# Order of two early loads and number of first spins in a fused cosine attention and MLP kernel

## The chip, the core and the metric

The kernel runs on one core of a Trainium2 chip. A core has four compute engines with instruction streams of their own: TensorE (PE; its weight loads are listed as PEld), VectorE (DVE), ScalarE (ACT) and GpSimd (POOL). SyncE (SP) only issues transfers. Each engine takes its instructions in the order in which the program issued them. Transfers run on the core's 16 DMA engines, whoever issued them. Those that POOL issues form the software queue, q0 in the profile; those of SP form a hardware queue, q1. The metric is the device time of one execution in microseconds (us), and smaller is better.

## The reference

Cosine attention over 8 batches with 12 heads, 448 positions and a head width of 64, then an MLP with the exact GELU:

```
q_n = q / (norm(q) + 1e-6);  k_n = k / (norm(k) + 1e-6)
scores = q_n @ k_n^T / tau            # tau = 0.1
attn = softmax(scores);  x = attn @ v # heads side by side: 3584 x 768
out = gelu(x @ w_in) @ w_out          # w_in 768 x 2048, w_out 2048 x 768
```

All inputs and the output are float32.

## The kernel before

Four heads of one batch make a quad; each batch has three quads, and there are 24 in all. For a quad, q and k come in as one tile of 448 KB each (`load_qk`, issued on SP, L129). Their squares are taken (`square`, L154 on ACT or L156 on POOL), summed over a head's width on VectorE (`reduce`, L165), turned into inverse norms (`logs` and `roots` on ACT, `inverses` with `rn` on VectorE, L192), and q and k are scaled by them into the bf16 tile `qkb` (`scale`, L208, mostly on POOL). `qkb` has to be transposed for the scores. The first five units (those of batch 0 and the first of batch 1) are transposed on PE into PSUM (`transposes`, tile `tp`, L225) and copied out by VectorE (`copies`, L230). From batch 1's second quad on, a DMA transpose issued by SP does it (L220). Then come the scores (`scores`, tile `st`, L246, PE), their exps (`exps`, tile `pt`, L253, ACT), the row sums and the products with v (`sums` L266 and L275, `values` L289, PE), and the division on VectorE that leaves `x` (L297 to L323). The exps need no maximum, since a cosine over tau is at most 10.

The MLP follows batch by batch. `first(b)` (L648) multiplies x by w_in (tile `hp`, L660) and ACT applies GELU (L695). The second product, with w_out (tile `op`, L352), is cut into single matmuls by `second_pieces` (L343). They are put into a list, `fill`, and `attention(b, fill)` (L596) takes them out in runs between the attention steps of the next batch; for batch 1 the runs are 20, 13, 14, 17, 16 and 16 matmuls long. For batch 0 the list is sorted so that the first 48 matmuls need only columns 0 to 383 of w_out, and the next 48 only columns 384 to 767.

Quad 0 is split into two units of two heads, so that its first scores can start before the rest is loaded. v comes in parts: quad 0 alone, quads 1 and 2 together, and then batch by batch (`load_v`, L137, transfer in L141). w_in comes in four blocks of rows and columns, each as two transfers (`load_wi`, L382, transfers in L387). Its first block holds rows 0 to 255 with all columns. w_out comes in four quarters (`load_wo`, L391, transfer in L394). All of these convert float32 to bf16 on the way, and POOL issues them all. Each `upto(f, n)` issues those of the first n calls of f that have not been issued yet.

The order of the first batch is written out by hand in `attention_first` (L411). It decides the order of each engine's instructions, and for POOL also when each load is issued. `spin(n)` (L406) issues n matmuls of a blank tile that nobody reads; they keep PE at work where it would wait. A spin uses the same PSUM tiles, in turn, as the transposes (`mm_tile`, L99), so a spin behind the transposes waits until the copy has read that tile. The 20 spins of L721 are the first PE work, ahead of the first transposes.

One load is held back by hand. In `first(0)`, behind the sixth GELU, POOL copies one column of the first tile that a DMA transpose has filled (`held`, L706 and the line behind it), and only then issues the last quarter of w_out (rows 1024 to 2047 of columns 384 to 767).

The lines around the change are these; quad 0's first unit is `0` and k is part `1`:

```python
        scale(0, ((DV, 1),))
        scale(0, ((GP, 0),))
        reduce(1, K)
        transposes(0, 1)
        upto(load_wi, 1)
        transposes(0, 0)
...
        copies(0, 0)
        upto(load_v, 2)
        roots(1)
```

Of the kernel before, what the change touches and what calls it, by code (L numbers as in the profile page):

```python
# [16 lines left out]
def kernel(  # L17
# [81 lines left out]
    def mm_tile(name, shape=(128, 512), dtype=F32, aside=None):  # L99
        t = ps_mm.tile(list(shape), dtype, tag=f"mm{turn[0] if aside is None else turn[0] ^ aside}", name=name)  # L100
        if aside is None:
            turn[0] ^= 1
        return t
# [54 lines left out]
    def reduce(u, part=slice(0, 2)):  # L158
        g, s0, s1 = units[u]
        sq = sq_t[g][:, :, s0:s1]  # L160
        n, j = place[u]
        if n not in nq_t:
            nq_t[n] = nrm.tile([128, len(groups[n]), 2, s1 - s0, C], F32, tag="nq", name=f"nq{n}")
        nq = nq_t[n][:, j]
        nc.vector.tensor_reduce(nq[:, part], sq[:, part], mybir.AxisListType.X, ALU.add)  # L165
# [8 lines left out]
    def roots(n):  # L174
        ln = ln_t.pop(n)
        if n <= NQ:
            sr_t[n] = root2[n % len(root2)][:, :math.prod(shapes[n])]
            nc.scalar.activation(sr_t[n][:, :, 0], ln.rearrange("p j i s c -> p (j i s c)"), AF.Exp, scale=0.5)
        else:
            sr_t[n] = nrm.tile(list(ln.shape), F32, tag="sr", name=f"sr{n}")  # L180
            nc.scalar.activation(sr_t[n], ln, AF.Exp, scale=0.5)  # L181
# [32 lines left out]
    def transposes(u, i=None):  # L214
        g, s0, s1 = units[u]
        qkb = qkb_t[g]
        if g not in qkT_t:
            qkT_t[g] = qkTp.tile([128, 2, C, 128], BF16, tag="qkT", name=f"qkT{g}")
        if i is None:
            nc.sync.dma_start_transpose(out=qkT_t[g].rearrange("p i c s -> p (i c) s"),  # L220
                                        in_=qkb.rearrange("p i c s d -> p (i c s d)"))
            return
        tp = tp_t[u, i] = mm_tile(f"tp{u}_{i}", (128, C, 128), BF16)
        for c in range(C):
            nc.tensor.transpose(tp[64 * s0:64 * s1, c, :], qkb[:, i, c, s0:s1].rearrange("p s d -> p (s d)"), ident)  # L225

    def copies(u, i):
        g, s0, s1 = units[u]
        rows = slice(64 * s0, 64 * s1)
        nc.vector.tensor_copy(qkT_t[g][rows, i], tp_t.pop((u, i))[rows])  # L230
# [169 lines left out]
    def upto(f, n, last=None):  # L400
        last = {load_qk: NG, load_v: NV, root: len(groups), load_wi: NQ + 1, load_wo: 4}.get(f, NU)
        while done.get(f, 0) < min(n, last):
            done[f] = done.get(f, 0) + 1
            f(done[f] - 1)

    def spin(n):  # L406
        ps = ps_mm.tile([128, 512], F32, tag=f"mm{turn[0]}", name="spin")
        for _ in range(n):
            nc.tensor.matmul(ps[:, :S], lhsT=ident, rhs=blank, start=True, stop=True)  # L409

    def attention_first():  # L411
# [15 lines left out]
        scale(0, ((GP, 0),))  # L427
        reduce(1, K)
        transposes(0, 1)
        upto(load_wi, 1)  # L430
        transposes(0, 0)
        logs(1)
        copies(0, 1)
        square(2, ((AC, Q),))
        copies(0, 0)
        upto(load_v, 2)
        roots(1)
        square(2, ((AC, K),))
        inverses(1)
# [278 lines left out]
    upto(load_qk, 1)  # L718
    nc.scalar.preload_act_table_set(EXP_SET)
    upto(load_qk, 3)  # L720
    spin(20)  # L721

    late = nrm.tile([128, 1], F32, tag="late", name="late", bufs=1)
    nc.gpsimd.tensor_copy(late, qk_t[0][:, 1, 1, C - 1, D - 1:D])
# [3 lines left out]
    for b in range(B):  # L728
        if b == 0:
            attention_first()  # L730
            acc.close()
            third.append(ctx.enter_context(tc.tile_pool(name="ps_third", bufs=1, space=bass.MemoryType.PSUM)))
        else:
            attention(b, fill)
        first(b)
        sb, hf = divmod(b, 2)
        todo = [(t, ni) for t in (range(3) if hf == 0 else range(3, 7)) for ni in range(2)]
        if b == 0:
            todo.sort(key=lambda x: x[1])
        tail = [2 * S // 128 - 1] if b == B - 1 else []  # L740
        fill = [f for t, ni in todo if t not in tail for f in second_pieces(sb, t, ni)]
        fill += [f for t in tail for f in last_pieces(sb, t)]
# [37 lines left out]
```

## Time and profile before

| | |
|---|---|
| median of 4 runs | 414.2 us (414.04 to 414.36) |
| the profiled execution | 414.23 us, one of these runs |
| its span, first to last instruction | 412.4 us |
| ACT busy, share of the span | 248.5 us, 60% |
| POOL busy, share of the span | 167.4 us, 41% |
| granted PE clock, mean over the span | 1.00 |
| time to landing, v of quad 0 | 7.7 us |
| time to landing, v of quads 1 and 2 | 15.5 us |
| time to landing, w_in's first block, two transfers | 8.1 and 10.6 us |
| time to landing, last quarter of w_out | 8.2 us |

The profile is one execution of the program on the chip. A row of its timeline has the start, the time, the engine, the line and the operation, the tiles that are written and read, the shapes, and how many such instructions follow each other. In brackets stands how long the engine had been idle before them, and what released it. An engine name with a q at its end (SPq) is the sequencer, which issues transfers. A row of the chain has the start, the time and what was done; the chain is followed back from the last instruction, at each step to what released it. A row of the DMA queues has the number of packets, the megabytes and the share of the 16 engines' time in the window that was asked for. A share above 100% means that packets overlap on an engine.

The time to landing runs from the start of the issue to the end of the transfer. Matmul ends are modelled, so the starts of matmuls are the better guide.

### The profile page before, as it was taken

How to read it: one execution, taken by the hardware profiler on the slowest of the kernel's cores; microseconds unless marked ns; L12 is line 12 of the kernel's file. 1: busy time of each engine (PE TensorE's matmuls, PEld its weight loads, DVE VectorE, ACT ScalarE, POOL GpSimd, SP SyncE). 2: the span in 40 equal slices, each digit the busy share in tenths (PEclk: the TensorE clock that was granted, in tenths of full speed). 3: DMA queues.
4: the chain of work that ended last, by engine and by line, in shares of the span. 5: the costliest groups of instructions: out<-in, count | busy, mean ns of one | idle time of the engine just before them, and what ended most of it. 6: DMA issues, size and time to landing. Idle time of an engine off the chain costs nothing.

```text
span 412.4 us, 8277 instructions
## 1 busy us (share of the span) xinstructions
PE 406.2 (98%) x3505; PEld 212.5 (52%) x3505; DVE 189.0 (46%) x381; ACT 248.5 (60%) x364; POOL 167.4 (41%) x116
## 2 busy tenths in 40 slices
PE   7999999999999999999999999999999999999996
PEld 3445555555555555555555555555555555555564
DVE  5785316931278222943158331773128611481021
ACT  5996696577656567664664658646665457754300
POOL 4995655093900928053720628227360233000000
PEclk9999999999999999999999999999999999999999
DMA  8999999852495507943495332965088130610033
GB/s 287 262 256 213 202 197 288 210 134 46 83 241 166 135 0 115 276 77 121 36 230 185 79 95 52 217 185 133 2 150 212 38 46 2 121 40 2 0 78 77
DMA packets 66484, 54.53 MB, mean 132 GB/s; under 512 B 38672, under 2 KB 62352, under 8 KB 66448
## 3 DMA queue, kind: packets, MB, share of 16 engines
q1 hardware_dynamic: 54464, 41.79, 40.1%
q0 software_dynamic: 11600, 11.80, 18.1%
q8 instruction: 27, 0.44, 0.4%
q10 hardware_dynamic: 384, 0.43, 0.3%
q14 instruction: 9, 0.07, 0.1%
HBM read 45.61 MB, written 11.01 MB: 137 GB/s over the span
## 4 chain that ended last, share of the span: by engine, by line
PE 95%; POOL 2%; DMA 1%; DVE 0%; ACT 0%; issue 0%; POOLq 0%
PE hp L660 35%; PE op L352 35%; PE st L246 9%; PE o L289 8%; PE sm L275 4%; PE op L371 1%; PE sm L266 1%; POOL qkb L208 1%; DMA qk<-in_q_dram 1%; PE tp L225 1%; POOL wi L387 1%; DVE nq L165 0%; PE spin L409 0%; POOL v L141 0%; ACT sq L154 0%
## 5 line engine op out<-in xcount | busy, mean ns | idle before, releaser
L253 ACT ACTIVATE pt<-st 128x896 bf16<-128x896 f32 x168 | 142.7, 916 | 65.9 <-PE st L246 65.5
L352 PE MATMUL op<-wo,g 128*128 128x384 bf16 x864 | 147.8, 327 | 0.0
L660 PE MATMUL hp<-x,wi 128*128 128x448 bf16 x768 | 146.9, 353 | 0.0
L352 PEld LDWEIGHTS <-g 128*128 128x128 bf16 x864 | 81.5, 98 | 62.0 <-issue 10.6
L660 PEld LDWEIGHTS <-wi 128*128 128x128 bf16 x768 | 74.4, 98 | 71.4 <-issue 3.0
L695 ACT ACTIVATE g<-hp 128x448 bf16<-128x448 f32 x128 | 65.4, 545 | 67.8 <-PE hp L660 67.6
L208 POOL TENSOR_TENSOR qkb<-qk,rn 128x896 bf16<-128x896 f32 (+1 forms) x49 | 79.6, 1647 | 40.7 <-DVE rn L192 40.7
L165 DVE TENSOR_REDUCE nq<-sq 128x28 f32<-128x1792 f32 (+2 forms) x30 | 48.7, 1634 | 50.4 <-POOL sq L156 47.7
L356 DVE COPY ot<-op 128x384 f32<-128x384 f32 x54 | 29.5, 547 | 88.0 <-PE op L352 86.0
L156 POOL TENSOR_TENSOR sq<-qk 128x1792 f32<-128x1792 f32 (+1 forms) x22 | 66.5, 3035 | 4.8 <-DMA qk<-in_k_dram 4.8
L190 POOL TENSOR_SCALAR se<-sr 128x28 f32<-128x28 f32 (+1 forms) x16 | 4.8, 298 | 125.8 <-ACT sr L181 125.8
L246 PE MATMUL st<-qkT 64*64 64x448 bf16 x672 | 47.5, 357 | 0.1
L289 PE MATMUL o<-pt,v 64*64 64x448 bf16 x672 | 37.7, 353 | 0.0
L192 DVE RECIPROCAL rn<-se 128x28 f32<-128x28 f32 (+2 forms) x20 | 7.1, 354 | 57.2 <-POOL se L190 57.0
L246 PEld LDWEIGHTS <-qkT 64*64 64x64 bf16 x672 | 18.6, 105 | 22.9 <-issue 14.3
L318 DVE STREAM_TRANSPOSE rs<-rc 128x448 f32<-128x448 f32 x48 | 28.4, 625 | 0.8
L323 DVE TENSOR_TENSOR x<-o,rs 128x448 bf16<-128x448 f32 x48 | 27.2, 599 | 0.6
L289 PEld LDWEIGHTS <-v 64*64 64x64 bf16 x672 | 17.7, 106 | 17.6 <-issue 9.0
L297 DVE STREAM_TRANSPOSE tr<-sm 128x448 f32<-128x448 f32 x24 | 15.5, 646 | 13.6 <-PE sm L275 11.1
L275 PE MATMUL sm<-pt,ones 128*32 128x448 bf16 (+1 forms) x336 | 17.8, 332 | 0.0
L309 DVE TENSOR_REDUCE tr<-tr 32x28 f32<-32x28 f32 x84 | 16.5, 196 | 1.6
L409 PE MATMUL spin<-blank,ident 128*128 128x448 bf16 x33 | 9.8, 447 | 2.2 <-DVE root L89 1.9
(44 smaller groups left out, 119.5 us busy)
## 6 DMA issues: line engine op xcount, KB each, us to landing
qk<-in_q_dram SPq DMA_DIRECT2D x23, 448.0 KB, 6.6
qk<-in_k_dram SPq DMA_DIRECT2D x23, 448.0 KB, 8.5
out_dram<-ot SPq DMA_DIRECT2D x48, 192.0 KB, 3.6
v<-in_v_dram POOLq DMA_DIRECT2D x7, 672.0 KB, 12.4
wo<-in_moe_w_out_dram POOLq DMA_DIRECT2D x4, 768.0 KB, 13.8
wi<-in_moe_w_in_dram POOLq DMA_DIRECT2D x4, 512.0 KB, 13.2
out_dram<-ot SPq DMA_DIRECT2D x12, 96.0 KB, 2.2
wi<-in_moe_w_in_dram POOLq DMA_DIRECT2D x4, 256.0 KB, 16.1
```

What stands on the lines that cost most here:

```text
L156: eng.tensor_tensor(sq[:, part], t[:, part], t[:, part], ALU.mult)
L165: nc.vector.tensor_reduce(nq[:, part], sq[:, part], mybir.AxisListType.X, ALU.add)
L208: eng.tensor_tensor(qkb[:, i, :, s0:s1].rearrange("p c s d -> p s c d"), t[:, i, s0:s1], rn[:, i].to_broadcast([128, s1 - s0, C, D]), ALU. ...
L246: nc.tensor.matmul(st[cols, n, :S], lhsT=qkT[rows, 1, c, cols], rhs=qkT[rows, 0, :, cols], start=True, stop=True, tile_position=(64 * s, 6 ...
L253: nc.scalar.activation(pt[:, :m], st[:, :m, :S], AF.Exp, scale=inv_tau)
L275: nc.tensor.matmul(bank_t[g, "sm"][r:r + 32, cols], lhsT=ones, rhs=pt_t[g, s, c][:, cols], start=(c < 2), stop=(c >= C - 2), tile_position ...
L289: nc.tensor.matmul(bank_t[g, h][cols, :S], lhsT=v_t[g][rows, s, c, :], rhs=pt_t[g, s, c][rows], start=(c == 0), stop=(c == C - 1), tile_po ...
L318: nc.vector.transpose(rs, bank_t[g, "rc"][:, h].to_broadcast([128, NB, 32]))
L352: nc.tensor.matmul(ps[:, :NH], lhsT=g_t[sb][:, kf, t * 128:(t + 1) * 128], rhs=wo[:, kf, ni * NH:(ni + 1) * NH], start=(kf == 0), stop=(kf ...
L356: nc.vector.tensor_copy(ot[:, ni * NH:(ni + 1) * NH], ps[:, :NH])
L660: nc.tensor.matmul(hps[m], lhsT=wi[:, kd, m * 128:(m + 1) * 128], rhs=x_t[b][:, kd, :], start=(kd == 0), stop=(kd == KD - 1))
L695: nc.scalar.activation(g_t[sb][:, m, hf * S:(hf + 1) * S], hps.pop(m), AF.Gelu)
```

## The change

Two lines of the hand-written program are different, in two places. In `attention_first`, the load of v for quads 1 and 2 is issued just ahead of the first block of w_in; before, it was issued three program lines behind the second transposes, and behind that block on POOL. In the body of the kernel the first burst of spins has 17 matmuls and not 20.

```diff
@@ attention_first
         reduce(1, K)
         transposes(0, 1)
+        upto(load_v, 2)
         upto(load_wi, 1)
         transposes(0, 0)
         logs(1)
         copies(0, 1)
         square(2, ((AC, Q),))
         copies(0, 0)
-        upto(load_v, 2)
         roots(1)
         square(2, ((AC, K),))
         inverses(1)
@@ body of the kernel
     upto(load_qk, 1)
     nc.scalar.preload_act_table_set(EXP_SET)
     upto(load_qk, 3)
-    spin(20)
+    spin(17)
```

Everything else is the same, on every engine.

## Prediction

> **What bounds the kernel now.** I read the page first: engine totals and the chain that ended last.
>
> ```profile
> span 412.4 us, 8277 instructions
> PE 406.2 (98%) x3505; PEld 212.5 (52%) x3505; DVE 189.0 (46%) x381; ACT 248.5 (60%) x364; POOL 167.4 (41%) x116
> ...
> PE 95%; POOL 2%; DMA 1%; DVE 0%; ACT 0%; issue 0%; POOLq 0%
> ```
>
> TensorE (PE) carries 95% of the chain. What another engine can still give lies at the start, so next I asked for the chain in order of time from 0 to 70 us.
>
> ```profile
> 6.97 1.36 POOL qkb L208
> 8.33 1.21 POOL wi L387 x2
> 9.54 0.78 POOL v L141
> 10.32 0.30 issue
> 10.66 1.83 POOL qkb L208 x2
> 12.49 1.20 POOL wi L387 x2
> 13.86 1.70 POOL qkb L208
> 15.60 0.56 PE tp L225 x7
> ```
>
> Up to 15.60 the chain is GpSimd's (POOL's); from there it is PE to the end. POOL stood still from 10.32 to 10.66, and again for 0.16 us before 13.86 (both times until VectorE's `rn`, says the timeline). Then the timeline from 0 to 11 us, engine by engine, for who holds `rn`:
>
> ```profile
> 1.93 6.49 PE L409 MATMUL spin<-blank,ident 128*128 128x448 bf16 x20 [1.93 <-DVE root L89]
> 8.47 0.94 PE L225 MATMUL tp<-ident,qkb 128*64 128x128 bf16 x14
> 9.06 1.15 DVE L230 COPY qkT<-tp 64x896 bf16<-64x896 bf16 x2 [1.00 <-PE tp L225]
> 10.87 0.92 ACT L253 ACTIVATE pt<-st 128x896 bf16<-128x896 f32 x1 [0.68 <-PE st L246]
> ```
>
> PE is in the spins until 8.42 and transposes at 8.47, although VectorE had the scaled k at 7.54 (row 6.91 + 0.63) and POOL the scaled q at 8.33. VectorE waits 1.00 us for the transposes, ScalarE (ACT) 0.68 us for the scores behind them. In the windows view ACT is then busy 20.79 of the 21.46 us from 10.87 to 32.33, so a microsecond gained at its first exp is nearly a microsecond gained at 32.33, where the w_in products start.
>
> **The change, part by part.** *Three spins fewer.* The weight loads of the spins start 0.37 us apart up to 7.11; the last five take 0.87 us together, 0.19 each. The three that go are of the fast kind: 3 x 0.19 = 0.57 us. The transposes of k start at 7.90 (k is there since 7.54). Those of q could start at 8.29 and wait for POOL's 8.33, so they begin near 8.38 and end near 8.93 instead of 9.41 (14 take 0.94, seven 0.55). The two copies (1.15) start when the first seven are out, 8.49, and run to 9.64 instead of 10.21. Spins and scores behind them move with them, and the first exp starts at 10.87 - 0.57 = 10.30. Its cover holds: ACT's own work before it ends at 10.19 (9.26 + 0.93), so of the 0.68 us idle 0.11 stays.
>
> Next is the chain through POOL. `rn` of the second half-quad comes 0.57 earlier, at 10.00, but POOL issues DMAs until 10.33 in either order, so its scaling starts near 10.37: 0.29 us gained. It ends at 12.20, the next two w_in issues at 13.40; `rn` of quad 1 is there at 13.77 - 0.5, so that scaling starts at 13.42 instead of 13.86: 0.44 gained, and PE's 15.60 becomes 15.16. ACT keeps between 0.44 and 0.57. I carry **0.50 us earlier at 32.33**, with ends of 0.3 (POOL's first step alone) and 0.57 (the spins' own length).
>
> *v ahead of w_in.* Three instructions on POOL change places (v 0.80, w_in 0.66 and 0.60); all three stay between the scaling that ends at 8.33 and the one that waits for `rn`, so POOL's time is the same, 2.05 us, and nothing of SP's or ACT's queue is passed. What changes is the order in the software DMA queue. By issue time plus time to landing: v of quad 0 lands at 5.48 + 7.7 = 13.2, w_in's two halves at 8.28 + 8.1 = 16.4 and 8.9 + 10.6 = 19.5, v of quads 1 and 2 at 9.53 + 15.5 = 25.0. So w_in takes 6.3 us of the queue and v 5.5. Exchanged, v lands near 18.7 and w_in near 25.0; what is behind stays. PE first loads this v at 25.72: 0.7 us of margin now, 0.2 with everything 0.5 earlier and the old order, over 6 with the new. w_in's first block is used at 32.33, 31.8 then: 6.8 us of cover. This edit costs nothing and alone gains nothing; it guards the first. Without it, v would just hold. The following block of w_in lands at 13.1 + 18.4 = 31.5 and is needed by the third w_in matmul at 32.7 - 0.5 = 32.2; the one after at 17.8 + 17.5 = 35.3 against 36.1 - 0.5 = 35.6. Both hold by 0.3 us or more.
>
> *What is late next.* From 32.33 PE runs without a wait until 63.5. There is one place where it meets a transfer just in time: the last quarter of w_out.
>
> ```profile
> 45.96 4.33 SPq L220 DMA_TRANSPOSE qkT<-qkb  x1
> 55.03 0.18 POOL L707 CAST held<-qkT 128x1 f32<-128x1 bf16 x1 [5.97 <-DMA qkT<-qkb]
> 55.27 0.96 POOL L394 DMA_DIRECT2D wo<-in_moe_w_out_dram  x1
> 60.58 2.27 SPq L220 DMA_TRANSPOSE qkT<-qkb  x1
> 62.04 2.96 PE L352 MATMUL op<-wo,g 128*128 128x384 bf16 x17
> ```
>
> By the fill's counts (20 + 13 + 14 of the 48 products that need the first two quarters) the first of these 17 ends that half, and the tenth is the first that needs the last quarter: 62.04 + 9 x 0.164 = 63.5. This w_out quarter takes 8.2 us to land, so it is there at 55.27 + 8.2 = 63.5 too. Margin: none. Does it move with PE? Its issue waits for the first DMA transpose, which lands at 45.96 + 9.0 = 55.0. That transpose starts when POOL has scaled, which follows PE and will be 0.5 earlier; but the software queue has run without a break since v (DMA share 1.27 from 32 to 52 us), and it is the backlog of it that the transpose has to share the engines with. The windows of DMA queues from 51 us: 42 software packets in one us beside 331 of the transpose, then 27 beside 231, then 5 beside 591, and alone 560 transpose packets in half a us. Starting earlier, the transpose meets 0.5 us more of a backlog whose own end is fixed by its bytes; the sum of the work ends when it did. I take the landing at 55.0 unchanged; ends: 0.5 earlier (it moves whole) and 1.5 later (the 130 packets more of backlog hold the transpose to the 231 per us of the slow rows for the 737 small packets that it sent in the window from 53.5 to 54.5, when the backlog was gone: 737/231 = 3.2 us, begun 0.5 earlier, in place of 1.2).
>
> And the second DMA transpose, issued at 60.58, moves 0.5 earlier into w_out's own tail. Windows 60.5:61.5, 61.5:62, 62:62.5 and 62.5:63:
>
> ```profile
> q0 software_dynamic: 259, 0.20, 127.9%
> q0 software_dynamic: 93, 0.06, 84.4%
> q0 software_dynamic: 16, 0.01, 17.5%
> q0 software_dynamic: 7, 0.01, 9.8%
> ```
>
> Alone the queue moves 259 packets a us; once the transpose's data come (from 61.7) it falls to 16 and 7 in half a us. Half a us earlier, 130 packets more are left: 8 on each of 16 DMA engines. Alone they would take 0.5 us, and w_out lands as before; at the pace of the last row, if it is two engines' (3.5 each in half a us, 0.14 us a packet), 8 take 1.15 us and it lands 0.65 later. I take 0.3 later, between them. By round-robin with one transpose packet (16/1120 = 0.014 us) to each of its own (16/259 = 0.062 us), 8 would take 0.61 us: 0.1 later.
>
> The Trainium skill, "DMA: Bandwidth & Descriptors", section "Queues, rings and completion order", has each DMA engine going round-robin between queues a packet at a time. By that rule alone the landing would slip by that 0.1 us; the rows of 62 to 63 us show a steeper fall.
>
> Sum: PE reaches the tenth product at 63.0 instead of 63.5 and waits for 63.8: +0.3 us on the span, 412.4 + 0.3 = 412.7. The profiled execution took 414.23, 1.83 more than its span; that is also the median of the runs (414.2) to 0.03. **414.5 us.** Behind 65 us nothing but PE's own work is on the chain, so what is lost there is not won back.
>
> **Rivals.** *The gain is kept* (414.23 - 0.5 = 413.7): the first DMA transpose lands 0.5 earlier, w_out is issued and lands with it. For it: every step from the w_in products to the transpose's issue follows PE. Against it: 9.0 us to landing where those at 86.0 and 93.5, with the software queue empty, take 4.0.
>
> *Slower* (the other side): the first DMA transpose lands later than now, because it meets a deeper backlog. With the 1.5 us above, w_out is issued at 56.8 and lands at 65.0 plus 0.3 for the second collision; PE is held to 65.3 instead of 63.5, +1.8, 416.0. Half of that gives 415.1: it decides from a transpose landing at about 55.6. For it: 231 packets per us under contention against 1120 alone. Against: the engines are not idle there (share 1.3), so the work is only shifted.
>
> *The clock.* The spin starts go from 0.37 to 0.19 us apart at 7.11 and the granted clock is full from there. With 20 spins, five run after that; with 17, two. If the step came about 1 us later, 17 slow spins would end at 1.93 + 17 x 0.37 = 8.2 with the clock still at half, and the sparse PE work after them (14 transposes 0.77, two spins 0.38, four scores 0.38) could run at half: up to 1.5 us more, about 1.0 of it on the path to the first exp; 0.5 late instead of early, and w_out then isn't the limit: 414.7 to 415.2.
>
> The Trainium skill speaks against the change here: "TensorE: Matmul & The Clock Gate", Part 1, says that the window that watches activity is free-running, so the step comes at another point in other runs, and Part 4 that transposes don't count as busy work in the same way. This trace shows one step, at 7.11, and says nothing of its spread; by the rule the 17 spins might now and then be too few.
>
> *It does nothing*: the copies are held elsewhere and ACT starts at 10.87 as now: 414.2. The rows leave no other releaser than PE, so this is small.
>
> **Chances.** Given back at w_out (414.1 to 414.9): 0.50. Gain kept (413.6 to 413.9): 0.17. Slower by the deeper backlog (414.9 to 416.0): 0.22. Clock: 0.07. Nothing: 0.04. The range 413.6 to 415.6 holds the first two and most of the others. 0.2% is 0.8 us, about what a measurement of this kernel can tell from no change; a gain above it would need more than the 0.57 us that the spins hold, so faster 0.05. Slower by over 0.2% is above 415.0: 0.18 of the backlog case, 0.05 of the clock, 0.06 from the upper end of the forecast: 0.29. The rest, 0.66, is within.
>
> **What will show it.** Right: 17 spins ending near 7.85, the copies at 8.5, ACT's first exp at 10.3 with about 0.1 us idle before it, PE's first w_in product at 31.8; v landing before 20, w_in's first block near 25; the w_out quarter issued at 55.3 again, landing after 63.5, and PE waiting 0.5 to 0.9 us for it in the run of 17. Wrong: no PE wait at w_out and a span near 411.9 (gain kept); the hold on POOL released at 56 or later (backlog); spin starts 0.37 apart to the end (clock); or the w_in products starting at 32.3 (nothing).

## The result, and the profile after

The changed kernel takes **417.95 us** in the median of 39 runs (415.79 to 422.42), the kernel before 414.37 us (60 runs). The ratio is 1.0069, 95% interval 1.0053 to 1.0085: **slower by 0.7%**, outside the predicted 413.6 to 415.6. The ratio compares all runs of the fast state; that of the two medians is 1.0086, because the changed kernel's median falls into the upper of two groups. Of its 39 times, 18 lie from 415.79 to 416.80, 17 from 417.71 to 418.54, and four from 421.38 to 422.42. The profiled execution took 417.99 us, so the profile below is of the second group; experiment 7 explains why there are two.

The page of the changed kernel gives the totals and the shares of the chain:

```profile
span 416.2 us, 8271 instructions
PE 407.6 (98%) x3502; PEld 212.4 (51%) x3502; DVE 189.1 (45%) x381; ACT 248.6 (60%) x364; POOL 167.5 (40%) x116
...
PE 90%; DMA 5%; POOL 2%; DVE 1%; issue 1%; ACT 0%; SPq 0%; DVEq 0%; POOLq 0%
```

No engine is busy for longer than before, except PE by 1.4 us. But the chain, 95% PE before, has 5% of DMA now. Its rows in order of time say which transfer (0 to 70 us, cut to the stretch that is new):

```profile
10.48 1.87 POOL qkb L208 x2
12.36 0.37 SPq L129
12.73 0.04 issue
12.78 16.70 DMA qk<-in_k_dram
...
35.49 0.29 POOL se L190
35.78 0.02 issue
35.80 0.33 DVE rn L192
36.13 0.52 DVE rs L318
...
36.74 0.62 DVE x L323
...
38.02 0.64 DVE x L323
38.65 0.04 issue
38.70 6.68 PE hp L660 x27
```

Here the loss begins. k of quad 4 (the fifth quad that SP loads; issued at 12.78) takes 16.7 us and lands at 29.47. In the kernel before, POOL squared this quad from 26.23 on (the third of the squares below) and had no wait; now it stands still. First come three rows of the kernel before, from the timelines of POOL and PE:

```profile
22.94 6.47 POOL L156 TENSOR_TENSOR sq<-qk 128x896 f32<-128x896 f32 x3
32.23 0.28 POOL L190 TENSOR_SCALAR se<-sr 128x28 f32<-128x28 f32 x1 [0.22 <-ACT sr L181]
32.33 9.25 PE L660 MATMUL hp<-x,wi 128*128 128x448 bf16 x48
```

The next three fences are of the changed kernel: POOL from 26 to 36 us, one row of VectorE, and PE from 31.5 to 39 us.

```profile
29.63 3.17 POOL L156 TENSOR_TENSOR sq<-qk 128x1792 f32<-128x1792 f32 x1 [3.71 <-DMA qk<-in_k_dram]
32.75 1.85 POOL L394 DMA_DIRECT2D wo<-in_moe_w_out_dram  x2
34.57 0.85 POOL L141 DMA_DIRECT2D v<-in_v_dram  x1
35.49 0.28 POOL L190 TENSOR_SCALAR se<-sr 128x28 f32<-128x28 f32 x1
```

```profile
35.80 0.33 DVE L192 RECIPROCAL rn<-se 128x28 f32<-128x28 f32 x1 [3.42 <-POOL se L190]
```

```profile
31.95 3.96 PE L660 MATMUL hp<-x,wi 128*128 128x448 bf16 x20
37.42 0.35 PE L660 MATMUL hp<-x,wi 128*128 128x448 bf16 x1 [1.51 <-DVE x L323]
38.70 0.53 PE L660 MATMUL hp<-x,wi 128*128 128x448 bf16 x1 [0.93 <-DVE x L323]
```

Read downwards: the square waits 3.71 us; behind it in POOL's queue stands `se` of quad 3 (35.49; before 32.23). VectorE's `rn` waits 3.42 us for `se`, and in VectorE's program `rn` stands ahead of the spreading and division of quad 2 (`x`, 36.74 and 38.02; before 33.56 and 34.84). The w_in products go through five column tiles on quads 0 and 1, 20 products, and the 21st is the first that needs quad 2. **PE waits for data that have nothing to do with the late transfer.**

The sum against the execution of before: the first w_in product comes 0.38 us earlier (31.95 against 32.33). The 22nd comes 38.70 - 31.95 = 6.75 us after it, 3.99 before: 2.76 lost. From there to the start of the 96th and last product of the run it takes 16.18 us against 14.78: 1.40 lost at a lower clock, which experiment 7 shows. 2.76 + 1.40 - 0.38 = 3.78, and the spans differ by 3.8.

Why is k late? Here are the rows of DMA queues from 17 to 23 us (packets, MB, share), of the kernel before:

```profile
q0 software_dynamic: 536, 0.68, 63.5%
q1 hardware_dynamic: 544, 0.92, 47.3%
```

and of the changed kernel:

```profile
q0 software_dynamic: 273, 0.99, 81.3%
q1 hardware_dynamic: 272, 0.46, 23.3%
```

In both, the two queues move **the same number of packets**, one for one, whatever their size. v goes in packets of 896 bytes, w_in in packets of 4096, q and k in 1792. Before, v's small packets were in the software queue while quad 4 came in on SP's. Now v has gone already, w_in's large packets are there, and SP's queue moves half as much (0.46 MB in place of 0.92). v's small packets now stand across from quad 3's load instead: its k lands at 15.59, before at 19.65. After that SP's queue is almost empty for a while, with 12 packets from 14 to 16 us.

### The profile page after: what moved, and what is told of

Same layout as the page of the kernel before. It is cut to its first block, busy times and chain, and to the rows that moved or that the text cites. A ratio compares the mean times of both kernels' runs of the same rounds, so it can differ in the third digit from the quotient of the medians.

```text
span 416.2 us, 8271 instructions
## 1 busy us (share of the span) xinstructions
PE 407.6 (98%) x3502; PEld 212.4 (51%) x3502; DVE 189.1 (45%) x381; ACT 248.6 (60%) x364; POOL 167.5 (40%) x116
## 4 chain that ended last, share of the span: by engine, by line
PE 90%; DMA 5%; POOL 2%; DVE 1%; issue 1%; ACT 0%; SPq 0%; DVEq 0%; POOLq 0%
PE op L352 35%; PE hp L660 35%; PE st L246 8%; PE o L289 7%; DMA qk<-in_k_dram 4%; PE sm L275 4%; PE op L371 1%; DMA qk<-in_q_dram 1%; POOL qkb L208 1%; POOL wo L394 0%; POOL v L141 0%; DVE x L323 0%; DVE nq L165 0%; DVE rs L318 0%; POOL wi L387 0%
## 5 line engine op out<-in xcount | busy, mean ns | idle before, releaser
L660 PE MATMUL hp<-x,wi 128*128 128x448 bf16 x768 | 148.6, 355 | 2.4 <-DVE x L323 2.4
```

The costliest lines, as they stand in the source:

```text
L660: nc.tensor.matmul(hps[m], lhsT=wi[:, kd, m * 128:(m + 1) * 128], rhs=x_t[b][:, kd, :], start=(kd == 0), stop=(kd == KD - 1))
```

## The experiments

The kernel before ran on the same chips: 414.03 us beside experiments 1 to 4, 414.49 beside 5 and 6 with its control and the failed run, 414.89 beside 7 to 9. In the diffs, minus and plus are against the changed kernel.

### 1. The spins alone

The old order with 17 spins: `upto(load_v, 2)` is back behind `copies(0, 0)`.

> Only the 17 spins; v stays behind w_in's first block. Theory S (the order of the loads is the cause: the k of quad 4 comes late, POOL's square waits for it, and everything behind that): the k of quad 4 lands near 25.7 us as before, POOL does not stand still ahead of its square, the first exp is at about 10.4 and PE's first w_in product at about 31.9 without a wait behind it. The time then follows the prediction's own sum: 413.7 if the w_out quarter moves along, 414.2 to 414.6 if it does not. Theory P (the earlier PE start is the cause, through the clock or through colliding transfers): the stall of some 3 us in the w_in products is here too, and the time is 416.4 to 418.2.

Measured: 414.00 us (12 runs), ratio 1.001 (0.9987 to 1.0033). Of the three spins neither a cost nor a gain can be told in the time. In the profile the gain is there at first: first exp at 10.22 (10.87), first w_in product at 31.73 (32.33). It is lost where the prediction said. PE from 60 to 65 us:

```profile
61.46 1.64 PE L352 MATMUL op<-wo,g 128*128 128x384 bf16 x9
63.59 1.46 PE L352 MATMUL op<-wo,g 128*128 128x384 bf16 x8 [0.49 <-DMA wo<-in_moe_w_out_dram]
```

The run of 17 is cut behind its ninth product: the tenth waits for the last w_out quarter, which lands at 63.55 (63.49 before).

### 2. The order alone

The new order with `spin(20)`.

> Only the order of the loads; 20 spins as before. Theory S: the k of quad 4 lands near 29.5 us, POOL stands still for about 3 us ahead of its square, PE waits about 2.4 to 3 us in the w_in products, and the time is 416.3 to 418.3, no better than with both edits. Theory P: no stall, 414.2.

Measured: 416.43 us (4 runs), ratio 1.0067 (1.0048 to 1.0086). The whole loss comes with the order. One of the four runs, 418.51 us, lies where the upper group of the changed kernel does. k lands at 29.14, and the rows of POOL and PE are the same two stalls:

```profile
29.30 3.17 POOL L156 TENSOR_TENSOR sq<-qk 128x1792 f32<-128x1792 f32 x1 [3.15 <-DMA qk<-in_k_dram]
```

```profile
37.08 0.35 PE L660 MATMUL hp<-x,wi 128*128 128x448 bf16 x1 [0.93 <-DVE x L323]
38.37 3.94 PE L660 MATMUL hp<-x,wi 128*128 128x448 bf16 x20 [0.93 <-DVE x L323]
```

Two steps of 1.28 us where 0.19 is normal cost 2 x 1.09 = 2.2 us, and the span is 414.5 against 412.4: 2.1 more.

### 3. The late load has nobody behind it

Both edits, and the square of quad 4 goes behind the scaling of quad 3, so that `se` and `rn` of quad 3 no longer stand behind it:

```diff
@@ attention_first
-        square(5)
         upto(load_wo, 2)
...
         scale(4)
+        square(5)
```

> Both edits, and POOL's square of quad 4 (the one that waits for the late k) moved behind its scaling of quad 3, so that nothing that the first batch needs is queued behind the wait. Theory S with its chain POOL square, POOL se, VectorE rn, VectorE x, PE: the k is as late as with the change (near 29.5), PE has no wait at its w_in products, and the time falls by 2 to 3.5 us to 413.7 to 414.7. If PE is held by something else that is late with the k (a transfer of its own, or PSUM), the stall stays and the time is 416 or more.

Measured: 414.02 us (11 runs), ratio 0.9999 (0.999 to 1.0007). k is as late as ever, 29.10, but POOL has done the rest first. POOL from 26 to 36 us:

```profile
25.69 1.85 POOL L394 DMA_DIRECT2D wo<-in_moe_w_out_dram  x2
27.51 0.85 POOL L141 DMA_DIRECT2D v<-in_v_dram  x1
31.69 0.28 POOL L190 TENSOR_SCALAR se<-sr 128x28 f32<-128x28 f32 x1 [3.33 <-ACT sr L181]
32.50 3.33 POOL L208 TENSOR_TENSOR qkb<-qk,rn 128x896 bf16<-128x896 f32 x2 [0.53 <-DVE rn L192]
35.80 3.17 POOL L156 TENSOR_TENSOR sq<-qk 128x1792 f32<-128x1792 f32 x1
```

`se` is back at 31.69, and PE runs 48 w_in products from 31.80 without a wait. So the late landing costs nothing by itself; the place of its user in POOL's queue costs the 2 to 4 us. This is the run that shows the cause.

### 4. v in the middle

Both edits, with v between the two transfers of w_in's first block.

> Both edits, but v goes between the two transfers of w_in's first block: behind the first, ahead of the second. Theory S in its sharper form (SP's queue must have run empty while v's small packets were served): here the load of quad 3 is still under way when v's packets come, so SP's queue is never empty, the k of quad 4 lands near 25.8 as before, v lands near 21, there is no stall, and the time is 413.7 to 414.6. If v ahead of any w_in does the harm by its place alone, the k lands between 26.5 and 29, and the time is 414.8 to 418.

Measured: 413.99 us (10 runs), ratio 1.0011 (0.9991 to 1.003). v lands at 22.58, k of quad 4 at 23.84, POOL never waits for it and PE has no stall. Only the place of v against w_in's transfers differs from the changed kernel, so the order of small and large packets sets k's landing.

### 5. Quad 4 loaded earlier

Both edits, with a fifth buffer for q and k, so that quad 4's load is issued at 5.58 and 6.74 instead of 12.36 and 12.78. It has three buffers fewer for the exps' results.

```diff
-    qkp = ctx.enter_context(tc.tile_pool(name="qkp", bufs=4))
+    qkp = ctx.enter_context(tc.tile_pool(name="qkp", bufs=5))
...
-    ptp = ctx.enter_context(tc.tile_pool(name="ptp", bufs=15))
+    ptp = ctx.enter_context(tc.tile_pool(name="ptp", bufs=12))
...
-    upto(load_qk, 4)
+    upto(load_qk, 5)
```

> Both edits, and a fifth buffer for the q and k tiles (three exp buffers fewer to make room), so that SP can issue the load of quad 4 at 5 us, right behind that of quad 3, and not at 12.3. Theory S in its sharper form (the k of quad 4 is late because SP's queue was empty while v's small packets were served, and then had to go packet by packet with w_in's large ones): the queue is no longer empty, the k lands by 21, nothing waits for it, and the time is 413.7 to 414.6. If w_in's large packets alone are the cause, whenever the load is issued, the k still lands after 26 and the time is 415 or more. Fewer exp buffers may cost PE or ScalarE some tenths of a us in the first batch.

A miss for my sharper theory, that SP's queue ran empty while v went in and so wasted the small packets. It was not empty here (323 software against 336 hardware packets from 13 to 16 us; 534 against 69 in the changed kernel), and k still landed at 30.53. From 20 to 24 us the counts are 181 and 183, again one for one and again against large packets. The queue as a whole was ahead, though. SP's loads up to quad 4 have 2432 packets of 1792 bytes; that many had gone in by 20.7 us (27.8 in the changed kernel, 22.9 in the kernel before). But part of quad 5's load, issued at 12.42, went in before quad 4's last packets: 2872 packets were in when quad 4's k landed, and 2541 in the changed kernel. So the empty queue may well have cost packets, and this run doesn't refute it. Why quad 4's last packets came so late stays open, since the trace doesn't tell which DMA engine carried what.

The time, 419.13 us (4 runs, ratio 1.0103, 1.0026 to 1.0179), says nothing of the order. PE waits seven times for exps here, 3.0 us in all, and not once in the changed kernel, probably for want of the three buffers. The profile is of the slowest of the four runs (424.02).

### 6. The last w_out quarter needed later, and its control

Old order, 17 spins, and the runs of w_out products for batch 1 cut so that the first product that needs the last quarter opens the fifth run and no longer stands tenth in the fourth; the control has the same runs and 20 spins.

```diff
@@ attention
-            parts = iter((20, 13, 14, 17, 16, 16) if b == 1 else (16, 14, 16, 18, 16, 16))
+            parts = iter((18, 12, 13, 13, 20, 20) if b == 1 else (16, 14, 16, 18, 16, 16))
```

> The old order of the loads, 17 spins, and batch 1's runs of w_out products cut as 18, 12, 13, 13, 20, 20 instead of 20, 13, 14, 17, 16, 16: the first product that needs the last quarter of w_out then stands in the fifth run, some 6 us later. If the gain of the three spins is given back at that quarter (the profile of the spins alone shows PE held there by 0.65 us), the wait is gone and the time falls by 0.3 to 0.6 us against the old kernel, to 413.4 to 413.7. If the gain is lost elsewhere, or is there only in some executions, the time stays at 413.9 to 414.1.

> The control for the run before: the old kernel with only the runs of w_out products cut as 18, 12, 13, 13, 20, 20. In the profile of the old kernel the wait at the quarter is 0.02 us, so nothing is to be won in executions like that one: 413.8 to 414.1. If the other cut itself costs something (PE waits for exps in the shorter runs), it shows here, above 414.1.

Measured: 415.63 us (12 runs, ratio 1.0022, 0.9982 to 1.0062) and 415.59 us (12 runs, ratio 1.0039, 0.9996 to 1.0082). No wait for the quarter is left, but both forecasts were missed. By the medians the new cut costs about 1.1 us (414.49 beside them), though both intervals include no change. In both profiles PE now waits 0.94 us for VectorE's copy of a w_out result. PE of the first kernel, 61 to 74 us (the control has the same row at 72.39):

```profile
71.98 0.85 PE L275 MATMUL sm<-pt,ones 128*32 128x448 bf16 x16 [0.94 <-DVE ot L356]
```

The medians are equal, though the profiled spans are 0.4 us apart (413.4 and 413.8). So whether 0.4 to 0.6 us can be kept behind w_out is not settled by this pair; it was too blunt a tool.

### The failed run: spins in the stall

To see whether PE's stall makes the clock fall, I put `spin(14)` in front of the 21st w_in product.

> Both edits, and 14 spins (2.65 us at 0.19) put into the stall of the w_in products, ahead of the first product that waits for quad 2's x. The stall itself stays, since it is not PE's: about 416.5 in every execution whose clock had not dropped before. If the second group of times with the change (418.0 to 418.5 beside 416.4 to 416.8) comes from the clock falling to half during the stall, that group is gone and the median falls from 418 to 416.4 to 416.8. If the two groups have another cause, both stay.

It failed as a test: 420.0 us (6 runs, ratio 1.011, 1.0049 to 1.0171). PE from 36 to 44 us:

```profile
38.24 2.81 PE L409 MATMUL spin<-blank,ident 128*128 128x448 bf16 x14 [2.52 <-DVE x L323]
40.88 3.38 PE L660 MATMUL hp<-x,wi 128*128 128x448 bf16 x17
```

The spins take a PSUM tile that the same late division had yet to read. They waited with everyone else and then ran 2.8 us in the way, so the run doesn't settle what it was made for.

### 7. Work in the stall that waits for nothing

The same 14 products, written into the bank of the fifth w_in tile, which is free; its first real product overwrites them.

```diff
@@ first, inside the loop that starts the first column tiles
             bank(m)
+            if b == 0 and m == ahead - 1:
+                for _ in range(14):
+                    nc.tensor.matmul(hps[m], lhsT=ident, rhs=blank, start=True, stop=True)
             mm(m, range(KD - 2))
```

> Both edits, and 14 blank products written into the fifth w_in tile's own bank ahead of its first real product in first(0), so that TensorE has work in the stall of the w_in run without needing a late tile (14 x 0.19 = 2.7 us, against waits of 1.51 and 0.93 us in the kernel after and 1.28 and 1.28 us with the order alone). What a blank product writes is overwritten by the tile's first real one. The k of quad 4 is as late as before (29 to 29.6), and the run is about as long as with the stall, since the blanks take what the waits took. Theory A (the group of times near 418 is the clock falling to half in that stall): no window between 36 and 44 us shows half the clock, and the group at 417.7 to 418.5 is gone; all times lie near 416.3 to 417.0. Theory B (the two groups have another cause, such as where the clock happens to be taken down later): both groups stay, 416.5 and 418.

Measured: 416.66 us, all 12 runs from 416.52 to 416.91. The windows from 36 to 42 us show the granted clock (PEclk, the last number but two); first the changed kernel, then this one:

```profile
36.00:38.00 2.00, 0.35 (x1) 0.10 (x1) 1.81 (x4) 0.00 (x0) 1.79 (x2) 1.00 1.25 193
38.00:40.00 2.00, 1.30 (x4) 0.54 (x4) 1.98 (x2) 0.00 (x0) 2.00 (x2) 0.54 1.31 203
40.00:42.00 2.00, 2.00 (x8) 0.79 (x7) 0.57 (x1) 1.47 (x4) 0.46 (x1) 0.60 1.31 204
```

```profile
36.00:38.00 2.00, 2.00 (x12) 1.02 (x11) 1.82 (x4) 0.00 (x0) 2.00 (x2) 1.00 1.31 208
38.00:40.00 2.00, 2.00 (x12) 1.06 (x11) 1.91 (x1) 0.64 (x2) 1.80 (x2) 1.00 1.31 205
40.00:42.00 2.00, 2.00 (x13) 1.00 (x11) 0.00 (x0) 2.00 (x5) 0.00 (x0) 1.00 1.33 208
```

Theory A holds: with PE kept at work the upper group (17 of 39 runs of the changed kernel) has no member left, and the lower group stays where it was. The mean granted clock of the changed kernel's runs agrees: 0.998 to 1.000 in the lower group, 0.994 to 0.996 in 16 of the 17 runs of the upper (1.000 in the one at 417.71). The kernel with the blank products was not run beside the changed kernel, and the kernel before was 0.5 us slower beside it than in the first comparison; that is too little to make up for two groups 1.7 us apart.

### 8. Half the packet

Both edits, with w_in's first block in four transfers of half rows, so that its packets have 2048 bytes.

```diff
@@ load_wi
-        for s in range(2):
+        for s, cols in [(s, c) for s in range(2) for c in ((slice(0, half), slice(half, d_ff)) if n == 0 else (cols,))]:
```

> Both edits, with w_in's first block issued as four transfers of half rows (2048-byte packets, twice as many) in place of two of whole rows (4096-byte packets): the same bytes in the same order, and two more issues on GpSimd, about 1.25 us, ahead of what it does next. If the two queues share by packets, one for one: quad 4's 512 packets get past w_in's in about half the bytes, k of quad 4 lands near 24 to 26 instead of 29.5, the square finds it there, no wait of TensorE in the w_in run, and 414.2 to 415.5 us (the later scaling costs up to 1 us). If they share by bytes or by time: k lands at 29 to 30.5 as in the kernel after, the square waits 3 us or more, and 416.5 us or more.

Measured: 415.21 us (10 runs), ratio 1.0014 (0.997 to 1.0059). The queues from 17 to 23 us, to be read against the two pairs of the first section:

```profile
q0 software_dynamic: 428, 0.84, 73.2%
q1 hardware_dynamic: 414, 0.71, 36.1%
```

The counts are equal again, at 0.71 MB for SP's queue: between 0.46 with w_in's whole rows and 0.92 with v. k lands at 27.37, POOL's square starts at 27.53 after a wait of 0.50 us, and PE has no stall in the w_in run. So the share goes by packets. The landing missed my 24 to 26. I had left out that with the two more issues on POOL SP's load is issued 1.1 us later too (second issue at 13.91, not 12.78), and that w_in's second block still comes in whole rows: from 23 to 26 us 138 software packets carried 0.49 MB, where 217 had carried 0.41 from 17 to 20. From issue to landing it is 13.5 us instead of 16.7. The first w_in product comes at 33.09, 1.3 later than the 31.80 of experiment 3, for those two issues, and that is the rest of the time.

### 9. Both mends

v between the transfers, 17 spins, and the square behind.

> v of quads 1 and 2 issued between the two transfers of w_in's first block (v of quad 1 and 2 late enough to pair with quad 4's load, early enough for its first product), 17 spins, and the square of quad 4 moved behind the scaling of the last quad. Theory (the whole loss is GpSimd's square waiting for k of quad 4): k of quad 4 near 24, no wait, 413.6 to 414.0 us, within 0.2% of the kernel before. Rival (something else of the new order costs as well, such as w_in's second transfer landing later): 415 us or more with waits of TensorE in the w_in run that no late square explains. A gain of over 0.2% (under 413.5) is expected by neither, since the last w_out quarter is where the first batch gives back what it gains.

Measured: 415.04 us (413.92 to 416.63, 12 runs), ratio 1.0003 (0.9974 to 1.0032): no difference from the kernel before, which took 414.89 beside it. The 413.6 to 414.0 of the forecast was missed in the number, but PE has no wait in the w_in run, which the rival needed. k lands at 23.98, and in the profile the 0.5 us gained at 31.83 goes into the wait for w_out's quarter (the tenth product at 63.39, 0.22 us idle). No version here beats the kernel before by more than its measurement can tell.

## Why the prediction was wrong, point by point

**Three spins fewer: right.** The rows of the changed kernel that answer to the spins, transposes and first exp of before (timelines of PE and ACT):

```profile
1.93 6.09 PE L409 MATMUL spin<-blank,ident 128*128 128x448 bf16 x17 [1.93 <-DVE root L89]
8.07 1.07 PE L225 MATMUL tp<-ident,qkb 128*64 128x128 bf16 x14
```

```profile
10.46 0.92 ACT L253 ACTIVATE pt<-st 128x896 bf16<-128x896 f32 x1
```

The 17 spins end at 8.02 (forecast 7.85), still later than the scaled k, because the clock became full at 7.45 here and at 7.11 before; the sum had taken 7.11 for fixed. The first exp, forecast at 10.30, comes at 10.46; in experiment 1, where the clock rose at 5.98 and PE even waited 0.25 us for the scaled k, at 10.22. The w_in products were to start 0.50 earlier: it was 0.38 and 0.60.

**v ahead of w_in: the step that failed**, as the prediction put it: "nothing of SP's or ACT's queue is passed", "what is behind stays", and so "This edit costs nothing". The runs showed in its place a k of quad 4 that lands 3.72 us later (29.47, before 25.75), a square that waits 3.71 us for it, and 2.76 + 1.40 us lost in the w_in products. The prediction reckoned the software queue alone, and there it was nearly right: v landed at 17.27 (forecast 18.7), w_in's block at 23.65 (25.0). But SP's queue runs beside it on the same engines, and what it gets depends on which packets stand across from it. Most of the size could have been worked out from the trace of before. Its queues moved equal numbers of packets, 536 and 544 from 17 to 23 us, and 0.27 MB/us together (0.24 in the changed kernel). Quad 4's load is 448 + 448 KB in 512 packets; with v gone, the 512 across from them are w_in's first two blocks, 2.1 MB. Together 3.0 MB at 0.24 to 0.27 MB/us are 11 to 12.5 us. Counted from the forecast's landing of v, 18.7, this estimate gives 30 to 31; from about 16, where these packets begin in the changed kernel, 27 to 28.5. It was 25.7 before, and 29.47 was measured. And the user's margin stood in the rows too: k landed at 12.93 + 12.8 = 25.7, and the square that needs it started at 26.2. It had half a microsecond, in a row where three squares follow each other without a break, so no wait pointed to it; with the spins alone the square already waits 0.49 us (experiment 1). I listed the next user of each transfer that I had moved, and not of those that I had not.

The Trainium skill, "DMA: Bandwidth & Descriptors", section "Queues, rings and completion order", says that each engine goes round-robin between its queues a packet at a time. The prediction quoted this for w_out's landing and used it there for 0.1 us; the packet counts of the three windows agree with it, and it is the rule that prices the step that failed.

**Late next, the w_out quarter: right in the profile of the spins alone.** The landing of the first DMA transpose was taken as unchanged, because the backlog of the software queue sets it. The runs fit that, though the loads in that queue are issued at other times in them too: issued at 45.35, 45.80, 45.96, 46.72, 48.01 and 49.75 (experiments 1 and 3, the kernel before, experiments 8 and 2, the changed kernel), it landed at 55.20, 53.86, 54.98, 54.47, 54.20 and 54.47. A start 4.4 us later makes no later landing. But the landings differ by 1.3 us, more than the 0.5 at stake. In the profiles of experiments 3 and 4, which have 17 spins too and are of the fastest run of each, the quarter lands at 61.22 and 62.77 and PE doesn't wait for it. So where the gain of the spins goes is shown for the profile of experiment 1, and not for every execution. The quarter itself was to be 0.3 later at 63.8 and came at 63.55, 0.06 later. The collision behind the 0.3 didn't come about: the second DMA transpose was to be issued 0.5 earlier and was issued at 60.67, before at 60.58. In the changed kernel nothing waits there, since PE comes 3.8 us late. POOL from 50 to 64 us:

```profile
54.52 0.18 POOL L707 CAST held<-qkT 128x1 f32<-128x1 bf16 x1 [1.67 <-DMA qkT<-qkb]
54.76 0.96 POOL L394 DMA_DIRECT2D wo<-in_moe_w_out_dram  x1
```

The quarter is issued at 54.76 (55.27 before), although PE and the transpose are 3.8 us later.

**The rivals.** The slower one had the right sign, at 415.1 to 416.0, for a reason that was not there: it needed the transpose's landing at 55.6 or later, and it was 54.47. The clock rival looked for half speed at the start; the clock did cost 1.4 us, but at 38 us, behind a stall.

## What to carry to other kernels

Before you move a transfer in one queue, list what the other queues move at that time. Here two queues shared by packets, so a large-packet transfer in place of a small-packet one halved what the neighbour got (0.46 MB, before 0.92). Then look for the neighbour's user with the smallest margin, to which no wait in the profile need point, and for what is queued behind that user. If a late transfer can't be avoided, put its user behind the work that the critical engine needs: here one moved line took back the whole loss.

## What the runs showed of the hardware

- Two queues with work move packets one for one: 536 and 544, 273 and 272, 428 and 414 in the same 6 us, for packets of mostly 896, 4096 and (at first) 2048 bytes in the software queue. The bytes of SP's queue went from 0.92 to 0.46 and 0.71 MB.
- Two waits of PE in a row, 1.51 and 0.93 us with one product between them, were followed in the changed kernel's profile by half the clock from 38.17 to 41.59 us. In experiment 5's profile waits of 2.10 and 0.93 us were followed by half the clock from 39.39 to 42.80. Two of 0.93 (experiment 2) left it full, and so did one of 2.52 in the failed run, so the length alone doesn't decide. The Trainium skill, "TensorE: Matmul & The Clock Gate", "Why this matters for your kernels", warns of idle gaps over about 3 us; here shorter ones were enough.
- What may decide is a grid in time. In all 13 profiles every later change of the clock lies a whole number of 3.413 us behind the moment when it first became full, 9 and 10 of them in the changed kernel, 10 and 11 in experiment 5. In the step just ahead of the drop PE was busy for 1.50 and 0.75 of the 3.41 us; the emptiest step behind which the clock stayed full has 1.71 (the failed run, where the wait of 2.52 was split between two steps). The grid begins at another time in each execution, so the same two waits can fall into one step or be split. That would give one kernel its two groups of times; no run tests it by itself.
- The time at which the clock first became full differed by execution, from 4.76 to 7.45 us, with the first matmul always at 1.93. With 17 spins the first exp came from 10.22 to 10.47 (11.00 in experiment 5), in no order with that time, since behind an early rise the transposes wait for the scaled k; with 20 spins from 10.73 to 10.87.
